# A conditioned linear-attention and MLP block on one core: a new written-out issue order and a new assignment of buffers and PSUM banks

## The chip, the cores and the metric

The kernel runs on one core of one Trainium2 chip. A core has five engines that run beside one another and meet by semaphores: TensorE for matrix products (PE in the profile, its weight loads PEld), VectorE (DVE), ScalarE (ACT), GpSimd (POOL) and SyncE (SP), which here does nothing but issue DMA transfers. The metric is the device time of the program in microseconds, median over the runs; lower is better.

## The reference

The block takes x of 2048 tokens by 512 channels, a condition vector c, and weights. A product of silu(c) with `w_mod` gives six rows of 512 (shift, scale and gate for each half). Cut to what matters:

```python
h = layernorm(x) * (1 + ca) + sa
q, k, v = split(h @ wqkv)                      # 32 heads of 16
phi(t) = [softmax(t @ w_phi), softmax(-(t @ w_phi))]    # 32 features per head
kv = phi(k)^T v ;  z = sum over tokens of phi(k)
o  = (phi(q) kv) / (phi(q) z + 1e-6)
x  = x + ga * (o @ wo)
h  = layernorm(x) * (1 + cb) + sb
x  = x + gb * (gelu(layernorm(h) @ w1 + b1) @ w2 + b2)
```

All in float32. The sums kv and z go over all 2048 tokens, so no token's attention output can be formed before the last token's k and v are known.

## The kernel before, in words

**Precision.** Each large product is made as three products of float32r parts: a high part and a remainder of both operands (function `mm3`). So every operand of a product has a second tile made by a subtraction, `hi` by ACT and `lo` by DVE or POOL.

**Stages.** Tokens are worked in eight blocks of 256, each in two tiles of 128.

1. Start: load the small constants (`blob`), x of blocks 0 and 1 (`xt`), `wkT`, `wqT` and the modulation weights `wm`. `silu_rows` makes the row tile `scp`; `fold_mm` folds `w_phi` into the k and q weights (products `fold`, read by `fold_out` into `wk`, `wq`); `mod_cols` makes the scale and shift columns (`prod`, `affine`); block 0 is transposed by TensorE (`hp`) and becomes `hT`.
2. Per block: products `pk`, `pv` and, for the first three blocks, `pq`. `k_chain` (DVE, ACT, POOL) turns `pk` into softmax features `ek`; `kv_mm` adds their products with `vf` to the bank `pkv`. From block 1 on, h is transposed through DRAM (`nb` to `nt_dram` to `hd`).
3. When all blocks are in: `kv_total` copies `pkv` to `kvT`, `z_total` makes `zp` and the tile `zb`, `kv_blocks` makes the block-diagonal kv.
4. Attention of a block: `attn_e` (features of q, tile `eq`), `attn_a` (`ez` = `eq` times `zb` on POOL, sums `dz`, reciprocals `rd`, then `eq` times `rcq` on POOL), a transpose (blocks 0 and 1 by TensorE products `qp`, items `t`; the others through DRAM, `eb` to `et_dram` to `eT`), products `po` (items `o`), products `pw` (items `w`), layer norms `ln_a`, `ln_b`, `ln_c` on DVE, ACT and POOL (items `la`, `lb`, `lc`), giving `h2`, and a second transpose (blocks 0 and 1 by products `yp`, items `y`; the others through DRAM, `yb` to `yf`), giving `yT`.
5. MLP, in four steps of 512 tokens: eleven products `pg` (item `u`: GELU and copy on ACT, subtraction on DVE, giving `g`), each followed by products into four banks `py0` to `py3` (item `d`), then the output. Attention of later blocks runs between them.

**What sets the order.** No scheduler runs at build time. Function bodies do not issue: a `Held` proxy puts each instruction into a queue of its item and engine (`Later.hold`). The table `ISSUE` then lists, string by string, which queue gives its next instruction (`Later.issue`): `k1.v` is the next DVE instruction of item k1, `+` and `-` name the next or the previous part of the program. Since every engine takes its instructions in the order of issue, the table fixes the order on each of the five engines, SP's DMA queue among them; the semaphore waits follow from the data and from which tile reuses which buffer. All instructions are issued by one line, L218 in the profile.

**Buffers.** `SLOTS["buf"]` says which of 19 equal SBUF buffers each of 284 work tiles uses, `SLOTS["bank"]` which of the eight PSUM banks each of 169 result tiles uses; the short strings choose among two or three copies of small tiles. A tile that reuses a buffer or bank waits until the last reader of the old tile is done. Where two engines read one bank, the one issued later waits for the other.

Of the kernel before, what the change touches and what calls it, by code (L numbers as in the profile page):

```python
# [65 lines left out]
    "den": "10000010",
    "rd": "11010110",
    "st6b0": "10111000",
    "stb0": "01010111",
    "veb0": "01100100",  # L70
    "rsb0": "01110010",
    "st6c0": "11010100",
    "stc0": "11001000",
    "vec0": "00110010",
    "rsc0": "11011010",
    "nmc0": "11110010",
    "st6b1": "11110111",
    "stb1": "00000011",
    "veb1": "10111001",
    "rsb1": "01101110",  # L80
    "st6c1": "11100001",
    "stc1": "01000010",
    "vec1": "10100011",
    "rsc1": "01000111",
    "nmc1": "11011001",
# [3 lines left out]
-init.v -init.v -init.p db.s x0.s x1.s dk.s dq.s dm.s si.a si.v dk.s si.v bd.v si.v dk.s sr.p dq.s s0.v s0.v s0.v  # L89
s0.v s0.v s0.v s0.g sr.a dm.s s1.v s1.v s1.v n0.v s1.v n0.v dm.s s1.v s1.v n0.v s1.g fk.p dm.s ok.a x.s fq.p n0.a  # L90
ok.v fq.p oq.a n1.v n1.v m.v m.g n1.a h0.p dk.s oq.v fk.p m.v m.a n1.v ++x.s fk.p oq.a f.v ok.a oq.v fq.p n1.a ok.v
fq.p f.a m.g m.v f.v h0.p m.v pf.p n1.v m.a m.g n1.s oq.a f.v ok.a dv.s m.v m.g f.a n1.s m.a f.v pf.p n1.s m.v m.v
oq.a n1.s m.a f.v dv.s fk.p m.v ok.v f.a bg.s f.v +x.s pf.p oq.v f.v s.v f.a ok.a f.v vs.a oq.v q0.p s.v s.v s.v s.v
ok.v n1.s q1.p bg.s s.v ++s.v s.g +bg.s vs.a vs.v vs.g n.v ++s.v n.a n.v pf.p n.a n.v n.v pv1.p bg.g ++s.v k0.v n.s
h.a q0.a +s.v n.s h.a +s.v n.s q1.a +bg.g +s.v ++s.v n.s ++s.v k0.v f.a pv0.p ++++x.s h.a +bg.v f.g +bg.s h.a +s.v
+s.v k0.v f.a +bg.s +s.v ++s.v +bg.s k1.v +s.g k1.v f.g
""",
    """
pk1.p n.v -k0.v n.a n.v +s.g e.v bg.a bg.g -k0.a +bg.s +++s.v -n.s pk0.p e.v ++x.s e.g bg.a -v1.a bg.g bg.v +n.v
+n.v k1.v bg.g bg.a -k1.v q0.p +n.a -k1.v +bg.g n.a bg.v +n.a n.v +bg.g +n.v pv1.p h.a k1.v h.a e.g +n.v +bg.a n.v  # L100
++++x.s bg.a e.g ++s.v h.a n.s q1.p -k0.v e.g h.a n.s q0.a n.s f.a ++s.v +n.s f.a f.g k1.v n.s +++s.v +n.s pv0.p
q1.a k0.v f.g e.a +bg.v ++s.v -k1.a k1.v +bg.s ++s.v ++s.v -k0.v -bg.a
""",
    """
pk1.p +++s.v --k0.g --v0.a +s.v ++s.v bg.v -n.s n.s -bg.v n.s +s.g -k0.v -v1.a pv0.p --v0.v --k1.v bg.g ++s.v +n.v
--v1.v bg.v +n.a +++s.v bg.a pv1.p --bg.v bg.a +n.v bg.v -k0.v +n.a e.v -k1.a n.s h.a ++s.v --k1.v pk0.p e.g h.a
k1.v f.a ++s.v --k1.g e.v h.a +++s.v +++s.v -k0.v q1.p f.g -k1.v -k0.a h.a --v1.v k0.v -v0.a +++s.v -v0.v --v0.v
k1.v f.a k1.v -m0.p f.g -m1.p +n.v bg.p q0.p +n.v e.g bg.a q1.a k0.v +n.s +h.a +++s.v k1.v +n.s +h.a +++s.g -k1.v
+n.s e.g v1.v
""",  # L110
    """
pk1.p -k0.v -bg.s -q0.a -e.g n.s -k0.v h.a -q1.s f.a --e.v --k1.g -k0.a -bg.s ----init.v --v1.v --e.a pk0.p n.s k1.v
# [12 lines left out]
""",
    """
pk1.p --k0.g h.a -k1.v -k0.v -k1.a --k1.g h.a -k1.v -v0.a pk0.p ----e.a -k0.v --bg.g f.a k1.v h.a -v0.v k1.v -k0.a
---v1.v -pv1.p k0.v h.a -k0.v f.g f.a +w1.s --bg.a -k1.v f.g -k0.v --v0.a
""",
    """  # L130
pk1.p -k1.v --k0.g ---v0.v --v1.v -k0.v -----e.v -k1.v --k1.g --m0.p -k1.a --m1.p k1.v -m0.p ---v1.v k1.v w1.s
--v1.a -pv1.p --bg.g -k0.v -----e.a -k0.v -k1.v -k0.a -k1.v pk0.p -----e.v -k1.g --v0.v -v1.v ---v0.v +a0.v -v1.v
pv0.p k0.v w1.a -k0.v -v1.a w1.g w1.a -----e.v -k0.v -m1.p k0.v m1.p w1.s w1.g pv1.p v1.v v1.v v0.v d0.s k0.v
-----e.s k0.v k1.v k0.a k1.v -k0.g d0.s v0.a k0.v -pv0.p k1.a v1.a +a0.g k0.v -v0.v k1.v k0.g q1.p -v0.a k1.v w1.a
+a0.v k1.g m0.p m2.p +a0.g m3.p d1.s kT.a +a0.g w1.s q1.a z.p +a0.a w1.g z.a kf.p q1.p z.a kf.v d1.s a0.g --bg.s
q2.p a1.g a0.v +a0.v q0.p a0.v +a0.g a1.v a1.g a0.v q2.p q2.a -v0.v a0.g a1.v a0.g q0.p a0.g a0.v a1.g a1.g a0.g
a1.g a0.g a1.v a0.v q0.a q4.p --bg.s w1.a a1.g +a0.a q1.a +a0.v t00.p a1.g q0.a t01.p t00.a q0.s t00.p +a0.v q4.a
t01.p q4.p a1.g v0.v t01.a q2.a t00.a t01.a +a0.g x0.s x1.s o00.p q2.s o01.p q1.s t10.p o00.a +a0.g t11.p o01.a
o00.v t10.p t11.a t11.p o01.v w00.p t11.a +a0.v t10.a -bg.g t10.a +a0.v o10.p la00.v o11.p +a0.g la00.a --bg.g w01.p
o10.a la00.v o11.a o10.v la00.v o11.v la00.v +a0.g la00.v +a0.g la00.g w2.s w11.p la01.v +lp1.s w1.g +a0.v la01.a  # L140
lb00.v la01.v lb00.v w10.p +a0.g la11.v la01.v lb00.v la11.a la01.v la01.v la01.g q4.a la11.v +a0.g q4.s lb01.v w1.s
q3.p la10.v lb01.v la10.a lb00.v la11.v lb01.v lb00.g la10.v la11.v lb01.v la10.v q3.p lc00.v la11.v lb01.g lc00.a
la11.g la10.v lc01.v la10.v lc01.a la10.g lb11.v +a0.g -bg.a lb10.v q3.a y0.p lb11.v y0.p y0.a lb10.v -bg.g y0.a
y0.v --bg.a y0.v
""",
    """
u0.p -lb11.v -w1.a -lb11.v -lb10.v a0.v -lb11.g u0.p a0.v -lb10.v -lc11.v a0.v a0.s -lb10.g -lc11.a -w2.g a0.s u0.p
-lc10.v a0.v -lc10.a a0.s a1.v -q3.a a0.s -y1.p a1.v a0.s -y1.p -y1.a u0.p -w1.g a0.s -y1.a -y1.v a0.s -y1.v a0.s
u1.p -q3.s ---bg.g u1.p u.a u.a a0.s u1.p u.v -w1.s u.a a1.g -w2.s u.a a0.s -w2.a a1.g d.p u.v d.p u.a a1.g u1.p u.a
a1.g d.p -w2.g a1.a d.p d.p a1.a a1.v d.p a1.g d.p a1.v d.p u.a u.v o00.p u.a a1.v o01.p -w1.a a1.g u.v u.p o01.a  # L150
+lp0.s x0.s o00.a o01.v a1.v -w2.g o00.v d.p a1.v d.p w00.p -w2.a a1.g +a0.v a1.g a1.g a1.v a1.g a1.g d.p la00.v
w01.p la00.a u.a la00.v a1.g +a0.v a1.v u.a d.p +a0.g a1.v d.p la00.v +a0.g a1.v a1.s d.p a1.v a1.s d.p +a0.g +a0.a
la00.v a1.s la01.v u.p la00.v a1.s la00.g la01.a +a0.g a1.s la01.v a1.s u.v -w2.g a1.s la01.v lb00.v d.p a1.s u.a
lb00.v d.p u.a la01.v la01.v d.p la01.g -w2.s u.p +a0.g lb01.v +a0.a a1.s u.v a1.s +a0.v x1.s -w1.g lb01.v d.p u.a
lb01.v lb00.v d.p lb01.v lb00.v +a0.v lb00.g -w2.s d.p -w2.s lb01.g d.p lc00.v -w2.g +a0.v lc00.a u.p u.a lc01.v
lc01.a u.v +a0.v -w2.a y0.v +a0.g o10.p u.a y0.v o11.p y0.s d.p o10.a y0.s o11.a o10.v d.p -w2.g y0.s o11.v w10.p
# [1013 lines left out]
```

## Time and profile before

| | |
|---|---|
| Median of the runs | 467.67 us (467.45 to 468.56, three runs) |
| Profiled execution, first to last instruction | 466.6 us; its own time is not given beside it, and the median is 1.07 us longer than this span |
| Granted TensorE clock | 1.000 |
| PE busy | 458.5 us, 98% of the span, 3297 instructions |
| DVE, POOL, ACT busy | 317.1, 279.7, 234.6 us |
| DMA | 68.05 MB, mean 146 GB/s |

A busy engine in the profile is one with an instruction in flight. For PE this overlaps: a 128x512 product is listed with 391 ns, but twelve of them follow one another in 2.72 us. So the share of PE says that it is rarely without work, not how much could be saved in it; the list of its waits says what it stood still for. The waits of the other engines cost nothing unless PE comes to wait for them.

### The profile page before, as it was taken

The numbers are of one execution on the slowest core, as the hardware profiler recorded it, in microseconds if no ns is written. First come the engines' busy times: TensorE is split into PE (matmuls) and PEld (weight loads), VectorE is DVE, ScalarE is ACT, GpSimd is POOL, SyncE is SP. The second block draws the span as 40 slices with busy tenths as digits, with TensorE's granted clock in tenths as the row PEclk, the third lists the DMA queues.
The fourth block names the chain that finished last, engine by engine and source line by source line (L and its number), as shares of the span: only waits on it lengthen the run. The fifth ranks groups of instructions, "written<-read, shape, count | busy, mean of one in ns | idle before, by whom it ended". The sixth has DMA issues, their size and how long they took to land.

```text
span 466.6 us, 8536 instructions
## 1 busy us (share of the span) xinstructions
PE 458.5 (98%) x3297; PEld 372.3 (80%) x3297; DVE 317.1 (68%) x612; ACT 234.6 (50%) x381; POOL 279.7 (60%) x233
## 2 busy tenths in 40 slices
PE   8999999999999999999999999999999999999996
PEld 5887888888878878978787878787788788788884
DVE  5999999989938599389797579896484472221113
ACT  4757866767440827848537743176133234422221
POOL 2369587999799998989899684756721020300000
PEclk9999999999999999999999999999999999999999
DMA  8998738492372664836837728077445504000003
GB/s 311 382 311 301 195 84 276 95 269 55 100 257 95 189 209 90 244 104 139 224 135 160 225 53 241 1 130 178 143 90 136 122 14 93 15 30 1 1 1 135
DMA packets 83673, 68.05 MB, mean 146 GB/s; under 512 B 54688, under 2 KB 70960, under 8 KB 83376
## 3 DMA queue, kind: packets, MB, share of 16 engines
q1 hardware_dynamic: 83632, 67.50, 50.9%
q8 instruction: 26, 0.43, 0.4%
q14 instruction: 15, 0.12, 0.1%
HBM read 44.94 MB, written 22.55 MB: 145 GB/s over the span
## 4 chain that ended last, share of the span: by engine, by line
PE 85%; DMA 5%; DVE 4%; POOL 2%; issue 1%; ACT 1%; SPq 0%; DVEq 0%; POOLq 0%; ACTq 0%
PE py L218 25%; PE pg L218 24%; PE pv L218 8%; PE pk L218 8%; PE pw L218 8%; PE pq L218 7%; PE pkv L218 2%; DMA wm<-in_wmodT 2%; PE po L218 1%; DVE pw L218 1%; DMA eT<-et_dram 1%; DMA wms<-in_wmodT 1%; DMA xt<-in_x 1%; PE qp L218 1%; POOL w2a L218 1%
## 5 line engine op out<-in xcount | busy, mean ns | idle before, releaser
L218 PE MATMUL pg<-yT,w 128*128 128x512 f32 (+1 forms) x528 | 115.3, 371 | 0.6 <-DVE yT L218 0.3
L218 PEld LDWEIGHTS pg<-yT,w 128*128 128x128 f32 x528 | 92.8, 188 | 18.5 <-DVE yT L218 0.5
L218 ACT ACTIVATE pg<-pg,blob 128x512 f32<-128x512 f32 x44 | 29.1, 662 | 100.6 <-PE pg L218 100.4
L218 PE MATMUL py<-w2a,g 128*128 128x512 f32 x288 | 70.7, 391 | 0.0
L218 DVE TENSOR_TENSOR g<-pg,g 128x512 fp32r<-128x512 f32 x40 | 27.2, 680 | 61.7 <-ACT g L218 61.7
L218 PEld LDWEIGHTS py<-w2a,g 128*128 128x128 f32 x288 | 53.6, 188 | 12.6 <-issue 1.6
L218 PE MATMUL pk<-wk,hT 128*128 128x512 f32 x192 | 46.2, 392 | 0.8 <-ACT hT L218 0.7
L218 PE MATMUL py<-w2b,g 128*128 128x512 f32 x192 | 46.9, 391 | 0.0
L218 PE MATMUL pv<-wvh,hT 128*128 128x512 f32 x192 | 45.9, 392 | 0.0
L218 PE MATMUL pw<-wo,oT 128*128 128x512 f32 x192 | 45.4, 390 | 0.0
L218 PE MATMUL pq<-wq,hT 128*128 128x512 f32 x192 | 45.3, 391 | 0.0
L218 PEld LDWEIGHTS pk<-wk,hT 128*128 128x128 f32 x192 | 35.6, 188 | 9.1 <-ACT hT L218 1.1
L218 PEld LDWEIGHTS py<-w2b,g 128*128 128x128 f32 x192 | 35.9, 188 | 8.1 <-issue 0.7
L218 PEld LDWEIGHTS pw<-wo,oT 128*128 128x128 f32 x192 | 35.9, 188 | 7.8 <-issue 0.4
L218 PEld LDWEIGHTS pv<-wvh,hT 128*128 128x128 f32 x192 | 35.7, 188 | 7.5
L218 PEld LDWEIGHTS pq<-wq,hT 128*128 128x128 f32 x192 | 35.8, 188 | 7.3
L218 POOL TENSOR_TENSOR ez<-eq,zb 128x1024 f32<-128x1024 f32 x15 | 36.8, 2469 | 5.5 <-ACT last L218 3.0
L218 POOL TENSOR_TENSOR yT<-yf,yT 128x256 fp32r<-128x256 f32 x24 | 17.2, 742 | 35.1 <-ACT yT L218 35.0
L218 POOL TENSOR_TENSOR ek<-ek,rck 128x1024 f32<-128x1024 f32 x16 | 30.8, 1939 | 4.5 <-DVE rck L218 2.3
L218 POOL TENSOR_TENSOR eq<-eq,rcq 128x1024 f32<-128x1024 f32 x15 | 28.9, 1937 | 0.3
L218 ACT ACTIVATE g<-pg 128x512 fp32r<-128x512 f32 x40 | 24.0, 599 | 9.5 <-PE pg L218 4.4
L218 DVE TENSOR_REDUCE smq<-eq 128x64 f32<-128x1024 f32 x16 | 19.2, 1207 | 6.8 <-ACT eq L218 6.8
(153 smaller groups left out, 783.4 us busy)
## 6 DMA issues: line engine op xcount, KB each, us to landing
et_dram<-eb SPq DMA_DIRECT2D x48, 128.0 KB, 2.9
eT<-et_dram SPq DMA_DIRECT2D x12, 512.0 KB, 5.1
xt<-in_x SPq DMA_DIRECT2D x8, 512.0 KB, 6.1
wms<-in_wmodT SPq DMA_DIRECT2D x8, 512.0 KB, 5.9
x<-in_x SPq DMA_DIRECT2D x8, 512.0 KB, 5.2
out<-x SPq DMA_DIRECT2D x15, 256.0 KB, 2.5
nt_dram<-nb SPq DMA_DIRECT2D x28, 128.0 KB, 3.4
hd<-nt_dram SPq DMA_DIRECT2D x7, 512.0 KB, 5.5
```

The source lines that it names most:

```text
L218: return lambda *a, **k: self.later.hold(self.letter, lambda: f(*a, **k))
```

## The change

Only the tables `SLOTS` and `ISSUE` change. The functions, the operations, their shapes, their engines and the number of buffers stay. The build of the change has the same products in number and size; their order, that of the other engines' instructions and of the DMA issues is new throughout, and so are nearly all buffers and banks. Its description: same operations; order of issue and buffers worked out anew by a search that knows PSUM readers, measured landings and rows of small products.

```diff
 SLOTS = {
...
     "bank":
-    "1264710140570135353253136162435026621304533162143502472521023727652170445605353123554624602715375317"
-    "153573175304761253153253215213576546037217123132712723327513246406462",
+    "0264053314155425735412536467370270221442034761733163556365177342730773725615173601336026023171451745"
+    "514174546406415225332755375372361602361271477554171417636207331133131",
...
 ISSUE = [
     """
-init.v -init.v -init.p db.s x0.s x1.s dk.s dq.s dm.s si.a si.v dk.s si.v bd.v si.v dk.s sr.p dq.s s0.v s0.v s0.v
+-init.v x0.s -init.v -init.p db.s x1.s dq.s dm.s dk.s dk.s dk.s dk.s s0.v si.a dm.s si.v si.v s0.v s0.v dq.s s0.v
...
-+a0.v k1.g m0.p m2.p +a0.g m3.p d1.s kT.a +a0.g w1.s q1.a z.p +a0.a w1.g z.a kf.p q1.p z.a kf.v d1.s a0.g --bg.s
+m3.p q1.p kT.a d1.s -bg.g d0.s z.p +a0.g z.a +a0.g kf.p z.a q1.p kf.v q1.a a0.g q2.p q1.a a1.g a0.v ----v1.v a0.v
```

Three places in the order, before and then in the change.

SP, the first rows of its DMA queue (`blob` the small constants, `xt` a block of x, `k` and `q` the weights to fold, `wm` the modulation weights, `wv_s` the v weights). Before:

```order
L218 DMA blob<-in_small 128x217
L218 DMA xt<-in_x 128x2x512 x2
L218 DMA k<-in_wkT 128x512
L218 DMA q<-in_wqT 128x1024
L218 DMA wm<-in_wmodT 128x1024
L218 DMA k<-in_wkT 128x512 x2
L218 DMA q<-in_wqT 128x1024
L218 DMA wm<-in_wmodT 128x1024 x3
```

The change:

```order
L216 DMA xt<-in_x 128x2x512
L216 DMA blob<-in_small 128x217
L216 DMA xt<-in_x 128x2x512
L216 DMA q<-in_wqT 128x1024
L216 DMA wm<-in_wmodT 128x1024
L216 DMA k<-in_wkT 128x512 x4
L216 DMA wm<-in_wmodT 128x1024
L216 DMA q<-in_wqT 128x1024
L216 DMA wm<-in_wmodT 128x1024 x2
```

The constants now go behind the first block of x, the first half of the q weights goes ahead of all k weights, and the four pieces of the k weights go ahead of the second `wm`. On PE the first fold products are accordingly those of q.

PE, where block 0 is transposed for the MLP (`yp`), between the last `pw` products and the first `pg`. Before:

```order
L218 MATMUL pw<-wo,oT_470 128x512
L218 MATMUL pq<-wq,hT 128x512 x24
L218 MATMUL yp<-blob,h_438 128x128 x8
L218 MATMUL pg<-yT_475,w_376 128x256
L218 MATMUL pg<-yT_477,w_376 128x256
```

The change:

```order
L216 MATMUL pw<-wo,oT_470 128x512
L216 MATMUL pq<-wq,hT 128x512 x12
L216 MATMUL yp<-blob,h_438 128x128 x8
L216 MATMUL pq<-wq,hT 128x512 x12
L216 MATMUL pg<-yT_475,w_376 128x256
L216 MATMUL pg<-yT_477,w_376 128x256
```

Twelve of the twenty-four `pq` products moved from ahead of the transposes to behind them. In the same way, as the two `m3.p` lines of the diff show, twelve `pq` products (`q1.p`) now stand between the last `pkv` products and `zp`.

POOL, from the attention of block 0 to the last `eq` times `rcq` of block 1 (`ez` are the products with `zb`, `dz`, `den` and `rcq` the small steps of the denominators). Before, from the third `ez` on:

```order
L218 TENSOR_TENSOR ez<-eq,zb 128x1024
L218 TENSOR_TENSOR dz<-dz,rcq 128x128
L218 TENSOR_TENSOR den<-dz 128x64
L218 TENSOR_TENSOR den<-den,deps 128x64
L218 TENSOR_TENSOR dz<-dz,rcq 128x128
L218 TENSOR_TENSOR den<-dz 128x64
L218 TENSOR_TENSOR rcq<-rcq,rd 128x128
L218 TENSOR_TENSOR den<-den,deps 128x64
L218 TENSOR_TENSOR eq<-eq,rcq 128x1024
L218 TENSOR_TENSOR rcq<-rcq,rd 128x128
L218 TENSOR_TENSOR eq<-eq,rcq 128x1024 x2
L218 TENSOR_TENSOR ez<-eq,zb 128x1024 x2
```

The change, from behind the third `ez`:

```order
L216 TENSOR_TENSOR dz<-dz,rcq 128x128
L216 TENSOR_TENSOR den<-dz 128x64
L216 TENSOR_TENSOR den<-den,deps 128x64
L216 TENSOR_TENSOR ez<-eq,zb 128x1024
L216 TENSOR_TENSOR dz<-dz,rcq 128x128
L216 TENSOR_TENSOR rcq<-rcq,rd 128x128
L216 TENSOR_TENSOR eq<-eq,rcq 128x1024
L216 TENSOR_TENSOR den<-dz 128x64
L216 TENSOR_TENSOR den<-den,deps 128x64
L216 TENSOR_TENSOR ez<-eq,zb 128x1024
L216 TENSOR_TENSOR rcq<-rcq,rd 128x128
L216 TENSOR_TENSOR eq<-eq,rcq 128x1024 x2
```

The two `ez` products of block 2, which stood behind the last `eq` times `rcq` of block 1, now stand ahead of it, on either side of the one of block 0. A subtraction `w_377` that stood ahead of the first `ez` has moved behind this piece.

More of the change, by code (lines that the diff above doesn't have):

```diff
@@ L82 @@
[L82 to L85, printed above, removed]
+    "0264053314155425735412536467370270221442034761733163556365177342730773725615173601336026023171451745"
+    "514174546406415225332755375372361602361271477554171417636207331133131",
+    "st6a": "00000000",
+    "sta": "00000100",
+    "vea": "00000000",
+    "rsa": "00001011",
+    "nma": "00000111",
+    "dz": "001111111",
+    "mxk": "1010111011101110",
+    "smk": "1000000000100101",
+    "rck": "0011001000100101",
@@ new lines @@
+    "mxq": "00001001",
+    "smq": "00000000",
+    "rcq": "01000000",
+    "den": "00000000",
+    "rd": "00000000",
+    "st6b0": "00000000",
+    "stb0": "00000000",
+    "veb0": "00000000",
+    "rsb0": "00000000",
+    "st6c0": "00000000",
+    "stc0": "00000000",
+    "vec0": "00000000",
+    "rsc0": "00000000",
+    "nmc0": "00000000",
+    "st6b1": "00000000",
+    "stb1": "00000000",
+    "veb1": "00000000",
+    "rsb1": "00000000",
+    "st6c1": "00000000",
+    "stc1": "00000000",
+    "vec1": "00000000",
@@ L86 @@
+    "rsc1": "00000000",
+    "nmc1": "00000000",
 }
@@ new lines @@
++a0.s d.p yf0.g yf1.a d.p yf1.a yf0.g yf1.a d.p out.v yf1.a d.p yf1.g d.p out.s yf1.g
+""",
+    """
+a0.s a1.a -yf1.g -yf1.g u.p a1.v a1.g u.p +a0.v u.a u.a +a0.v a1.g -out.v u.p a1.v u.a -out.s a0.s u.a a1.v -xb.g
+u.v d.p u.v u.a x0.s d.p a0.s u.a +a0.g d.p u.v d.p +a0.g a1.v d.p a0.s +a0.g +a0.a -out.v d.p +a1.v d.p xb.g a0.s
+d.p +a1.v d.p u.p a1.g a1.g a1.g a1.v a1.g +a0.g d.p u.a d.p u.a a1.g d.p u.v d.p -out.v +a0.a +a0.v o00.p a1.g
+o01.p +a0.v d.p o01.a d.p +a0.g o00.a +a0.v d.p a1.v u.p a1.v +a0.g +a0.v a1.s a1.s a1.v a1.s u.p u.a o01.v a1.s u.a
@@ new lines @@
+la10.v +a0.s d.p la10.v +a0.s la10.v la11.v d.p +a0.s la11.v u.p la11.v la10.v la11.g y0.s la10.g +a0.s lb10.v +a0.s
++a0.s lb10.v u.p lb10.v lb10.v lb10.g lc10.v la11.v lc10.a lb11.v u.a u.p u.a lb11.v yf0.a +a0.s lb11.v yf0.a lb11.v
+u.a lb11.g +x0.s xb.g lc11.v u.a u.v lc11.a u.v d.p y1.v d.p y1.v d.p +a1.g +a1.a y1.s d.p y1.s +a1.a d.p +a1.v
++a1.g y1.s d.p y1.s +a1.v d.p +o00.p u.a +a1.v +a1.g +o01.p u.a +a1.v d.p u.a u.a y1.s d.p u.a u.a u.a +x1.s +o00.a
+d.p u.v yf0.g +o01.a +o00.v d.p yf0.g yf0.a d.p +o01.v yf0.g d.p out.v d.p out.v +w01.p out.s out.v +a1.v yf1.a
@@ new lines @@
+yf1.a yf1.a yf1.a +a1.g yf0.a +w00.p +a1.g +a1.g yf1.g yf1.g yf1.g d.p +la00.v yf1.g out.v yf0.g
+""",
+    """
+u.p la00.v la00.v la00.v la00.v la00.v u.p la00.g u.a a1.v u.a a1.g u.v a1.g u.p u.a a1.g u.a u.v lb00.v u.p u.a
+lb00.v u.a lb00.v la01.v u.v la01.v d.p la01.v u.a d.p u.a la01.v a1.v d.p a1.v d.p a1.v a1.s d.p a1.v a1.s d.p
+-out.s u.v a1.s d.p la01.v la01.v la01.g a1.s d.p lb01.v a1.s d.p a1.s lb01.v d.p a1.s a1.s d.p d.p a1.s u.p a1.s
+d.p u.a d.p u.a d.p u.v d.p lb00.v lb00.g d.p lc00.v lb01.v lc00.a lb01.v d.p lb01.g d.p lc01.v y0.v lc01.a o11.p
@@ new lines @@
+yf0.a d.p yf1.g d.p yf0.g d.p d.p d.p out.v d.p out.v d.p out.s +u.p out.v -out.s out.v --out.s out.s out.s -out.s
+""",
+    """
+u.p -out.s u.a u.a u.v d.p u.a d.p u.a d.p u.v d.p u.p d.p u.a d.p u.a d.p u.v d.p d.p d.p d.p d.p u.p u.p u.a u.a
+u.v d.p u.a d.p u.a d.p u.v d.p d.p d.p u.p u.p u.a u.a u.v d.p u.a d.p u.a d.p u.v d.p d.p d.p d.p d.p d.p d.p u.p
+u.p u.a u.a u.v u.p u.a u.a u.v u.p u.a u.a u.v d.p u.a d.p u.a d.p u.a u.a d.p u.a u.a u.a d.p u.v d.p d.p d.p d.p
+d.p d.p d.p out.v d.p out.s d.p out.v ---out.s d.p out.s d.p out.v d.p out.s out.v out.v out.s out.s
```

186 lines of the change are left out of this document (68 added, 118 removed).

## The prediction

> **What bounds the kernel now.** I read the engine totals first, then the chain that ended last, then the list of what PE waited for.
>
> ```profile
> PE 458.5 (98%) x3297; PEld 372.3 (80%) x3297; DVE 317.1 (68%) x612; ACT 234.6 (50%) x381; POOL 279.7 (60%) x233
> PE 85%; DMA 5%; DVE 4%; POOL 2%; issue 1%; ACT 1%; SPq 0%; DVEq 0%; POOLq 0%; ACTq 0%
> 39.77 2.72 PE pq L218 x12
> ```
>
> PE is in 85% of the chain, and the third line, a piece of that chain, shows its pace: twelve products of 512 columns in 2.72 us. The change has the same products, so at this pace PE's work is the same, and a new order can gain only what PE now waits. That is the whole of this list (waited for: us in total, times, longest):
>
> ```profile
> PE warm L218 <- DVE mhalf L218: 0.9, 1, 0.9
> PE fold L218 <- DMA k<-in_wkT: 0.9, 1, 0.9
> PE pk L218 <- ACT hT L218: 0.7, 1, 0.7
> PE zp L218 <- ACT kvT L218: 0.6, 1, 0.6
> PE pg L218 <- DVE yT L218: 0.3, 1, 0.3
> PE pg L218 <- ACT yT L218: 0.3, 1, 0.3
> PE po L218 <- DMA eT<-et_dram: 0.2, 1, 0.2
> PE pk L218 <- POOL hT L218: 0.2, 1, 0.2
> ```
>
> The sum is 4.1 us. The first 0.9, ahead of the warming products, waits for the program's first memsets, which stay; 3.2 us are open to an order, 0.7% of the run. Against them stands that any of the many tight meetings of five engines may now miss. The two stretches where these are tightest, grouped (us, then PE, PEld, DVE, ACT, POOL busy with instruction counts, clock, DMA share, GB/s):
>
> ```profile
> 120.00:160.00 40.00, 39.45 (x518) 32.23 (x517) 25.13 (x34) 17.16 (x27) 36.95 (x26) 1.00 0.44 151
> 160.00:200.00 40.00, 39.12 (x274) 33.22 (x273) 31.36 (x63) 27.54 (x40) 37.27 (x30) 1.00 0.65 187
> ```
>
> POOL has only 3 us free in each 40, so here its order matters nearly as much as PE's. The clock is full, so no term below comes from it.
>
> **The change part by part. The start.** Issues, landings and first users (start, length, what; the last two rows are landing times of the two tiles, min/median/max):
>
> ```profile
> 0.74 0.40 SPq L218 DMA_DIRECT2D blob<-in_small  x1
> 1.19 4.54 DMA xt<-in_x
> 2.68 0.43 SPq L218 DMA_DIRECT2D q<-in_wqT  x1
> 2.85 0.21 ACT L218 ACTIVATE ex<-blob 128x4 f32<-128x4 f32 x1 [0.83 <-DMA blob<-in_small]
> 3.96 0.15 DVE L218 TENSOR_TENSOR sc<-blob,rx 128x4 f32<-128x4 f32 x1
> 5.76 1.29 DVE L218 BATCH_NORM_STATS2 st6a<-xt 128x6 f32<-128x512 f32 x2 [1.64 <-DMA xt<-in_x]
> 5.86 1.05 PE L218 MATMUL scp<-blob,sc 128*128 128x128 f32 x8
> 7.78 1.16 PE L218 MATMUL fold<-bd,k 128*128 128x128 f32 x8 [0.86 <-DMA k<-in_wkT]
> DMA to landing us min/median/max: 2.1/2.1/2.1
> DMA to landing us min/median/max: 6.3/7.3/8.3
> ```
>
> Before, `blob` lands at 0.74 + 2.1 = 2.8, and `sc` is ready at 4.1, well ahead of PE, which is warming until 5.86. In the change `xt` is issued first: it lands about 1.19 - 0.74 = 0.45 earlier, at 5.3, and `blob` behind it at about 5.5. From its landing to `sc` it took 4.1 - 2.8 = 1.3, and DVE now has one of the two statistics (0.65) in between: `scp` starts at about 7.4, a new wait of 1.5, and ends at 8.5. The first q weights landed at 2.68 + 6.3 = 9.0; without the k piece ahead of them they land at about 8.3, so the folds go on without another wait at 8.5, where before they began at 7.78: 0.7 lost. After that the four k pieces come in one row and the waits of 0.7 and 0.2 for `hT` should shrink, because `hd` of block 1 no longer stands behind three weight loads. But both `hp` tiles now share one bank, and the second must wait for the last reader of the first:
>
> ```profile
> 17.61 0.42 DVE hT L218
> ```
>
> That reader ended at 18.0 before; PE would want the bank at about 17.4. I take 0.7 lost + 0.2 for the bank - 0.9 of old waits = **0.0**, with -0.9 (blob is small and lands with xt) to +1.3 (both new waits in full, the old ones too) as bounds.
>
> **zp.** The twelve `pq` products put between `pkv` and `zp` last 2.72; what PE waited for is one ACT copy:
>
> ```profile
> 135.66 1.99 PE L218 MATMUL zp<-kvT,blob 128*128 128x256 f32 x8 [0.55 <-ACT kvT L218]
> ```
>
> It is covered four times over: **-0.6**. If the cover were gone, the 0.6 would be back.
>
> **The two `ez` ahead of block 1's last product.**
>
> ```profile
> 138.61 4.78 POOL L218 TENSOR_TENSOR ez<-eq,zb 128x1024 f32<-128x1024 f32 x2
> 153.91 3.83 POOL L218 TENSOR_TENSOR eq<-eq,rcq 128x1024 f32<-128x1024 f32 x2
> 157.70 4.72 POOL L218 TENSOR_TENSOR ez<-eq,zb 128x1024 f32<-128x1024 f32 x2
> 158.64 1.09 PE L218 MATMUL po<-qT,gab 64*32 64x256 f32 x32
> 159.67 1.97 PE L218 MATMUL qp<-blob,eq 128*128 128x128 f32 x16
> ```
>
> `eq` of block 1 was ready at 157.74 and PE transposed it (`qp`) at 159.67: 1.9 us of slack. Now 4.7 us of `ez` go first. PE comes sooner by the 0.6 of `zp` and by half of the `po` group (0.5), which goes behind the first transpose. If POOL gained nothing elsewhere, PE would wait 4.7 - 1.9 + 1.1 = 3.9 us, of which the 1.1 is only time already gained: net +2.8. On the other side POOL reaches `ez` earlier, since the 2.4 us subtraction `w_377` and others moved behind, and `zb` comes 0.6 sooner; then the slack nearly holds and the cost is 0. I take **+0.4**, nearer the second because the moved subtraction alone is half of the 4.7.
>
> **yp and the first pg.**
>
> ```profile
> 161.39 3.00 PE L218 MATMUL pw<-wo,oT 128*128 128x512 f32 x12
> 165.79 0.70 DVE L218 BATCH_NORM_STATS2 st6b<-pw 128x6 f32<-128x512 f32 x1 [0.66 <-ACT x L218]
> 176.46 1.62 ACT L218 ACTIVATE h<-pw,nmc,rsc 128x512 f32<-128x512 f32 x2 [1.11 <-DVE nmc L218]
> 179.08 1.04 PE L218 MATMUL yp<-blob,h 128*128 128x128 f32 x8
> ```
>
> From the end of the first `pw` (164.4) to the end of `h` (178.1) the layer norms took 13.7. In the change PE has 1.1 of `po`, three `pw` of 2.72 and one `pq` of 2.72 in that time, 12.0, so an unchanged chain would make `yp` wait 1.7. The chain is shorter now: DVE issues the statistics ahead of ACT's copy of the same bank, which saves the 0.66 shown, and block 1's first steps no longer stand ahead of block 0's last ones; I put it at 12.4, a wait of 0.4. Behind `yp` the other `pq` group covers both waits of `pg`, 0.6. **-0.2**, from -0.6 to +1.1.
>
> **eT of block 2.**
>
> ```profile
> 193.29 6.65 DMA eT<-et_dram
> ```
>
> Its second half stood on SP behind a `w1s` and a `ws` load; in the change the two halves are issued in a row, so 2 us of landing go. The DVE transposes that feed them now stand behind two subtractions for `yT`, which eats most of it. **-0.2**, to +1.0 if they are late.
>
> The MLP steps, where PE waited for nothing, get **0.0**. Sum: 0.0 - 0.6 + 0.4 - 0.2 - 0.2 = -0.6. The span of the profiled execution is 466.6, the median 1.07 longer; a wait that goes shortens both alike, so the forecast is 467.67 - 0.6 = **467.1 us**, no change that can be told: what a measurement of this kernel can tell from none is about 0.3%, 1.4 us.
>
> **The rivals.** *Nearly all waits go.* For it: each wait on PE's list has been given a visible cover, and my new waits come from landings put together by hand. Against it: the start's `blob`. Of the 3.2 us some 0.4 stays: 467.67 - 2.8 = 464.9.
>
> *Banks come back too soon, slower.* In the bank string, read along PE's order, an up product `pg` takes or gives a bank with only 2.72 us of other products between last write and reuse in ten places or more; before, in one. What must happen in that time:
>
> ```profile
> L218 ACT ACTIVATE pg<-pg,blob 128x512 f32<-128x512 f32 x44 | 29.1, 662 | 100.6 <-PE pg L218 100.4
> L218 ACT ACTIVATE g<-pg 128x512 fp32r<-128x512 f32 x40 | 24.0, 599 | 9.5 <-PE pg L218 4.4 <-POOL wlast L218 2.7 <-PE pw L218 1.3
> L218 DVE TENSOR_TENSOR g<-pg,g 128x512 fp32r<-128x512 f32 x40 | 27.2, 680 | 61.7 <-ACT g L218 61.7
> L218 ACT ACT_TABLE_LOAD x16 | 20.5, 1283 | 1.0 <-PEq L1163 0.7
> ```
>
> 0.66 + 0.60 + 0.68 = 1.94, so 0.8 is to spare: enough on an idle ACT, not when a table load of 1.28 stands ahead, which costs PE 0.5. The rival decides from the point where four of these places meet one: 4 x 0.5 = +2.0, 469.1 us. Queued behind the waiting `pg` are then all of PE and every later `py`. Against it: ACT is busy only half of the time. [...] No run so far shows a wait of this kind.
>
> *POOL is late.* The bound of +2.8 in place of +0.4 at `eq`: 467.1 + 2.4 = 469.5. It holds if POOL cannot fill earlier gaps.
>
> *The order does nothing*, new waits for old ones one for one: 467.7.
>
> **How the numbers follow.** Forecast 0.45, own range 466.0 to 468.4; a fifth of it (0.09) lies below 466.27, the rest (0.36) within 0.3%. Nearly all waits go: 0.28, faster. Banks: 0.12, slower. POOL: 0.09, slower. Nothing: 0.06, same. So faster 0.37, same 0.42, slower 0.21. The range, 464.6 to 469.6, takes in the rivals' times and leaves out a new stall of more than 2 us.
>
> **What would show it.** Right: no `zp` and no `pg <- yT` on PE's list; `scp` starting near 7.4; a wait of `qp` or its weight load for POOL `eq` under 1 us; PE's waits summing to about 3.5. Wrong: `scp` still at 5.9 and the list under 1.5 us (the gain), `pg`, `py` or `pw` waiting for DVE `g` or `x` in the MLP steps (the banks), or `po` waiting for `eT` after 200 us by more than 1 us at a time, which I have priced at nothing.

## The result, and the profile after

The changed kernel takes 478.21 us (median of four runs, 477.22 to 480.5); the kernel before took 467.96 us beside it (467.45 to 468.56). The ratio is 1.0228, with a 95% interval of 1.0201 to 1.0255: about 10 us slower, outside the range of the prediction and on the other side of its forecast. The profiled execution took 477.91 us, its span is 476.1 us, 9.5 more than before.

The same two lines of the page as quoted before, for the changed kernel: busy time per engine, then the share of each engine in the chain that ended last.

```profile
PE 461.0 (97%) x3297; PEld 372.7 (78%) x3297; DVE 323.1 (68%) x612; ACT 234.7 (49%) x381; POOL 280.3 (59%) x233
PE 69%; POOL 6%; DMA 3%; issue 2%; DVE 1%; SPq 1%; ACT 0%; DVEq 0%; POOLq 0%
```

The products are the same 3297, but PE's share of the chain fell from 85% to 69%: other engines now set the pace for part of the span. What PE waited for (us in total, times, longest):

```profile
PE pk L216 <- issue: 2.3, 1, 2.3
PE fold L216 <- DMA q<-in_wqT: 1.6, 1, 1.6
PE qp L216 <- POOL eq L216: 1.5, 1, 1.5
PE pv L216 <- issue: 1.5, 1, 1.5
PE po L216 <- DMA eT<-et_dram: 1.1, 2, 0.7
PE pkv L216 <- issue: 1.1, 1, 1.1
PE warm L216 <- DVE mhalf L216: 0.9, 1, 0.9
PE scp L216 <- PE warm L216: 0.6, 1, 0.6
PE pv L216 <- POOL hT L216: 0.3, 1, 0.3
PE pkv L216 <- POOL ek L216: 0.2, 1, 0.2
PE hp L216 <- DVE hT L216: 0.2, 1, 0.2
```

The list sums to 11.3 us against 4.1 before, +7.2. Three kinds of loss are in it. The largest, 4.9 us in three pieces, has "issue" as its releaser: PE waited for nothing that the profile shows. The start lost 1.3 (`fold` and `scp`, 2.2 against 0.9). `qp` waits 1.5 for POOL, and `po` 0.9 more for `eT`. Gone are, as predicted, the waits of `zp` (0.6) and of `pg` for `yT` (0.6); the 0.9 of `pk` for `hT` went too, and three small waits, 0.7 together, came. A fourth loss is not in the list but in the clock. The stretch behind the wait of `qp`, grouped (us, busy times, and the granted clock after the busy times):

```profile
160.00:168.00 8.00, 6.48 (x66) 4.72 (x64) 3.59 (x4) 3.00 (x6) 7.69 (x9) 1.00 0.70 244
168.00:172.00 4.00, 4.00 (x32) 3.51 (x17) 1.84 (x3) 2.63 (x5) 4.00 (x3) 0.57 1.05 389
```

The trace's record of the clock has 3.41 us at half clock there, and that gives a mean of 0.57 over 4 us. If PE does nothing but products in that time it loses by estimate half of the 3.41, 1.7 us; in the run with 108 below, twelve `pv` products that ran from 87.57 us over such a stretch took 4.60 us, where twelve at full clock take 2.88. With it the sum is 7.2 + 1.7 = 8.9 of the 9.5 us.

**The three stalls without a cause.** They all fall in or right behind rows of `pkv`, the small products. PE's timeline round the first (start, length, what, and the idle time before it):

```profile
108.48 2.88 PE L216 MATMUL pv<-wvh,hT 128*128 128x512 f32 x12
111.29 1.85 PE L216 MATMUL pkv<-ek,vf 128*17 128x32 f32 x192
115.44 1.88 PE L216 MATMUL pk<-wk,hT 128*128 128x512 f32 x7 [2.30 <-issue]
```

A row of 192 such products has as many weight loads, 384 instructions in 1.8 us, 4.7 ns each; twelve large products are 24 instructions in 2.72 us, 113 ns each. The page's list of DMA queues has one of the kind `instruction`:

```profile
q8 instruction: 26, 0.43, 0.4%
```

These are 26 transfers of 16 KB each, and PE's 6594 products and loads are 25.8 times 256. In the trace a transfer of this queue begins at 112.70, 130.91 and 135.82 us, each 0.2 to 1.0 us ahead of a stall. So I counted PE's products, loads and semaphore instructions in the order of the trace. The stalls come at the places 2241, 2753 and 3009, 512 and 256 apart, and I looked at every 256th place from them. This is my count, not a view of the profile:

```
place in    reached   us since the place   next instruction
PE's order  at, us    256 earlier          at, us
1729         99.92    4.2                   99.93
1985        111.82   11.9                  111.83
2241        112.95    1.1                  115.44   stall
2497        129.88   14.4                  129.88
2753        131.44    1.6                  133.33   stall
3009        136.84    3.5                  138.09   stall
before, the shortest: 2753 at 127.52, 3.8 us since 2497, no stall
```

All three stalls stand exactly at such a place, and only where 256 instructions were used up in 3.5 us or less; the next instruction came 3.45 to 4.8 us after the place before. In each of the three the next instruction came 2.3 to 2.7 us after the transfer had begun. In the kernel before, whose rows of `pkv` stand otherwise to these places, the shortest block of this stretch lasted 3.6 to 3.8 us (the count is good to one instruction, and one is worth 0.2 here), and it has no such stall. The theory for the experiments, an estimate from this table: PE's instructions come in blocks of 256, the next block is asked for when one has been begun, it takes about 3.5 us to come, and a block that lies wholly in `pkv` is used up sooner.

**Where POOL's lateness comes from.** PE at `zp` and at `qp`, and POOL's row between them, in the changed kernel:

```profile
141.73 1.89 PE L216 MATMUL zp<-kvT,blob 128*128 128x256 f32 x8
167.18 0.55 PE L216 MATMUL qp<-blob,eq 128*128 128x128 f32 x3 [1.52 <-POOL eq L216]
```
```profile
144.38 8.11 POOL L216 TENSOR_TENSOR ez<-eq,zb 128x1024 f32<-128x1024 f32 x3 [3.46 <-issue]
153.62 2.41 POOL L216 TENSOR_TENSOR ez<-eq,zb 128x1024 f32<-128x1024 f32 x1
160.42 2.41 POOL L216 TENSOR_TENSOR ez<-eq,zb 128x1024 f32<-128x1024 f32 x1
163.30 3.83 POOL L216 TENSOR_TENSOR eq<-eq,rcq 128x1024 f32<-128x1024 f32 x2
```

POOL stood idle 3.46 us until `zb` was there; this "issue" is a wait for the two ACT copies of `zp`, which ran from 142.8 to 144.3 (before, they ended at 138.3, 0.3 ahead of the first `ez`). The prediction's rows of before give the difference: `ez` begins at 144.38 instead of 138.61, 5.8 late; `eq` of block 1 ends at 167.1 instead of 157.7, 9.4 late, the other 3.6 being the two `ez` of block 2 that now go first. Of the 9.4 the old slack of 1.9 takes its part, and PE goes on at 167.18 instead of 159.67, 7.5 late. So the stalls are one part of a delay that runs through POOL, and PE's list of waits shows only where the parts come to the surface.

### The profile page after: what moved, and what is told of

Its sections match the earlier page's. It is cut to its first block, busy times and chain, and to the rows that moved or that the text cites. A ratio compares the mean times of both kernels' runs of the same rounds, so it can differ in the third digit from the quotient of the medians.

```text
span 476.1 us, 8581 instructions
## 1 busy us (share of the span) xinstructions
PE 461.0 (97%) x3297; PEld 372.7 (78%) x3297; DVE 323.1 (68%) x612; ACT 234.7 (49%) x381; POOL 280.3 (59%) x233
## 4 chain that ended last, share of the span: by engine, by line
PE 69%; POOL 6%; DMA 3%; issue 2%; DVE 1%; SPq 1%; ACT 0%; DVEq 0%; POOLq 0%
PE pg L216 23%; PE py L216 23%; PE pw L216 9%; PE pv L216 5%; PE pk L216 4%; POOL ez L216 3%; DMA eT<-et_dram 2%; PE pkv L216 2%; PE po L216 2%; POOL eq L216 1%; PE pq L216 1%; DMA et_dram<-eb 1%; POOL ek L216 1%; PE qp L216 1%; SPq L216 1%
## 5 line engine op out<-in xcount | busy, mean ns | idle before, releaser
L216 PE MATMUL py<-w2a,g 128*128 128x512 f32 x288 | 68.8, 390 | 0.0
L216 POOL TENSOR_TENSOR rsb<-veb,mhalf 128x1 f32<-128x1 f32 x16 | 8.7, 548 | 38.0 <-DVE veb L216 37.9
L216 ACT ACTIVATE h<-pw,nmc,rsc 128x512 f32<-128x512 f32 x16 | 12.3, 778 | 35.8 <-DVE nmc L216 27.2
```

The costliest lines, as they stand in the source:

```text
L216: return lambda *a, **k: self.later.hold(self.letter, lambda: f(*a, **k))
```

## The experiments

Each kernel has its own runs of the kernel before beside it; the ratios are to these. 1% is 4.7 us.

**Do the stalls follow the count?** In the kernel before the third warming product is replaced by tiny ones, so that all later PE instructions move by 108 or by 56 places and nothing else changes.

```diff
-    for _ in range(3):
+    for _ in range(2):
         nc.tensor.matmul(warm, ones.to_broadcast([P, P]), ones.to_broadcast([P, 512]), start=True, stop=True)
+    for _ in range(28):      # 15 in the other run
+        nc.tensor.matmul(warm[:32, :2], ones.to_broadcast([P, 32]), ones.to_broadcast([P, 2]), start=True, stop=True)
```

> The kernel before, with the third warming product (4 PE instructions, 1.7 us) replaced by 28 tiny ones (112 instructions): every later PE instruction stands 108 places further on, nothing else changes. Theory (blocks of 256 instructions): in the changed kernel PE stood still at instructions 2241, 2753 and 3009 of its stream, 256 or 512 apart, each time less than 1 us after a 16 KB transfer of the instruction queue had begun; between that point and the one 256 instructions earlier only 1.1, 1.6 and 3.5 us had passed, and the next instructions came 3.45 to 4.8 us after the earlier point. Worked out with 3.45 us for all of before's rows of pkv, this shift puts two block ends into four of its rows of 384 instructions: PE loses 11 us, 477 to 482 us. Rival (the stalls come from something else at those times, such as data or transfers): the tiny products are hidden at the start and the time stays within 1 us of before, 467 to 469.

> The same edit with 15 tiny products: every later PE instruction stands 56 places further on. Theory (blocks of 256 instructions): worked out the same way, no row of pkv then holds a whole block, so no stall: 467.5 to 468.5 us, as before. Rival (more instructions or a shorter warming cost by themselves, in proportion): about half of what the shift by 108 costs.

Measured: moved by 108, 488.47 us, ratio 1.0425 (1.0395 to 1.0455); moved by 56, 469.15 us, 1.0022 (1.0008 to 1.0037). The waits of the first:

```profile
PE pkv L218 <- issue: 11.0, 4, 3.9
PE po L218 <- DMA eT<-et_dram: 1.5, 1, 1.5
```

Four stalls of 11.0 us in sum, as worked out, at places 1472, 1984, 2496 and 3265 of the count, 256 or a multiple of it apart and, to one instruction, on the same grid as those of the changed kernel. The whole loss is larger, 20.5 us. Behind each of the four the granted clock was 0.57 to 0.59 over 4 us; the first of them:

```profile
84.00:88.00 4.00, 1.92 (x156) 1.69 (x142) 1.05 (x3) 4.00 (x8) 4.00 (x3) 1.00 0.02 4
88.00:92.00 4.00, 4.00 (x12) 3.12 (x11) 3.92 (x11) 1.97 (x3) 4.00 (x3) 0.57 0.50 80
```

Four times the estimated 1.7 us is 6.8; the tiny products also ran later than the one that they replaced (`scp` began at 7.7 instead of 5.9, 1.8 us). 11.0 + 6.8 + 1.8 = 19.6 of the 20.5. The shift by 56 has no stall and costs 0.2%, not half of the other, so the number of instructions is not the cause: where the blocks of 256 end is.

One part of the theory does not hold, that a block used up in less than 3.5 us always brings a stall. In the run with 108 the whole block of the places 705 to 960 is this row, used up in 1.26 us, and PE went on without a pause:

```profile
65.68 1.33 PE L218 MATMUL pkv<-ek,vf 128*32 128x32 f32 x128
```

There a 16 KB transfer had begun at 62.62, 3.1 us ahead of the block. At the four stalls the transfer began 1.0 to 3.0 us after the block had been begun. Over all stalls of this kind in these runs the next instruction came 2.2 to 2.8 us after the transfer's start, 3.6 in the one of `after_shift180` below. So the blocks are shown, by eight stalls in three kernels on one grid of 256 places (three in the changed kernel, four here, one in `after_shift180`), and the time from a transfer's start to the next instruction; what decides when a transfer starts stays open.

**Two parts of the change put into the kernel before.** First the twelve `pq` products between the last row of `pkv` and `zp`, then block 2's two `ez` ahead of block 1's last `eq` on POOL, then both.

```diff
 # PE
-pkv  zp  kvp  pq x12
+pkv  pq x12  zp  kvp
 # POOL
-eq<-eq,rcq x2  ez x2
+eq<-eq,rcq  ez x2  eq<-eq,rcq
```

> The kernel before with one part of the change alone: twelve pq products stand between the last pkv row and zp. Theory: zp no longer waits 0.6 to 0.7 us for kvT, but zb is ready 2 us later, so POOL's row to eq of block 1 ends 2 us later, and the 1.9 us of slack at qp are used up, PE being there 0.7 us sooner: a wait of qp of 0.5 to 1 us, total 467.5 to 468.5 us, no gain. Rival (my prediction's step: the cover is free): 467.0 to 467.4 us, no wait of qp.

> The kernel before with another part of the change alone: on POOL the two ez of block 2 (4.7 us) go ahead of block 1's last eq*rcq. Theory: POOL has no gap there, so this eq is ready 4.7 us later, at 162.4 instead of 157.7; PE wants it at 159.7: a wait of 2.7 us at qp and what follows from it, 470.5 to 472 us. Rival (POOL or the products around it make room): a wait under 1 us, 467.5 to 468.5.

> The kernel before with both parts of the change together: twelve pq products between the last pkv row and zp, and block 2's two ez ahead of block 1's last eq*rcq. Theory (one row of POOL work from zb to eq, in which delays add): eq of block 1 is ready 1.7 to 2 us plus 4.7 us later, about 164.3; PE comes to it at about 159.1 and waits 4.5 to 5.5 us, with 3.4 to 6.8 us at half clock behind it: 474 to 476.5 us. Rival (the two delays cover one another): no more than the larger of the two alone, 471 to 473.

Measured: `zp` late 470.05 us, 1.0049 (1.0028 to 1.0070); `ez` first 472.45, 1.0099 (1.0067 to 1.0131); both 473.65, 1.0111 (1.0093 to 1.0129). The wait of `qp` in the first, the second, and the third kernel:

```profile
PE qp L218 <- DVE eq L218: 1.9, 1, 1.9
```
```profile
PE qp L218 <- POOL eq L218: 2.5, 1, 2.5
```
```profile
PE qp L218 <- DVE eq L218: 1.9, 1, 1.9
PE qp L218 <- POOL eq L218: 1.2, 1, 1.2
```

`zp` no longer waits, and the kernel is about 2 us slower: what was won at `zp` (0.6) came back threefold at `qp`, 1.9, more than the 0.5 to 1 that I had put down, because DVE's `eq` of block 0 hangs on `zb` too and PE wants it first. The two `ez` bring a wait of 2.5 us, where the working gave 2.7. The profiled run of this kernel took 473.61 us, 5.9 more than the kernel before; the other 3.4 are by estimate what the clock behind the wait gives, 0.57 over 8 us, twice the length seen in the changed kernel:

```profile
161.00:169.00 8.00, 6.68 (x25) 5.98 (x26) 2.95 (x4) 2.17 (x4) 6.88 (x6) 0.57 0.49 183
```

Together the two parts cost no more than can be told from the larger alone: 1.11% against a sum of 1.48%. The first wait of 1.9 covers part of the second, 1.2 instead of 2.5. The theory that the delays add is wrong; the rival holds, and its 471 to 473 would be 472 to 474 against the 468.65 us of before in these runs.

**The stalls taken out of the changed kernel.** In two ways by breaking up the rows of `pkv`, once by a shift of 180 places ahead of them.

```diff
 # PE, after_split
-pkv x3 tiles  pk1  pk0  pv0  pv  pv  pkv x3 tiles  pv1  pkv x3 tiles
+pkv x1  pk1  pkv x2  pk0  pv  pv  pkv x2  pv0  pkv x1  pv1  pkv x3 tiles
 # PE, after_split2
+pkv x1  pk1  pkv x2  pk0  pv0  pv  pv  pkv x1  pv1  pkv x2  pq x12  pkv x3 tiles  zp
 # PE, after_shift180
+45 tiny products (180 instructions) into pv's bank ahead of the pv before the first of these rows
```

> The changed kernel with two places of PE's order altered so that no block of 256 instructions falls wholly into pkv products: the two pkv tiles of block 5 go behind the product pk1 of block 7, and pv0 of block 7 goes between the second and third pkv tile of the next row. Theory (blocks): the three stalls of 2.3, 1.7 and 1.2 us go, PE reaches zp about 5 us sooner; POOL, busy without a pause up to 140.9, follows by only some 3.5, so the wait of qp for eq grows from 1.5 by up to 1.7: 473 to 475.5 us. Rival (the stalls belong to that time or to the transfers in it): 477 to 479.

> The changed kernel with its last three pkv rows broken up in another way: pk1 of block 7 between the first and second tile of one row, pv1 of block 7 between the first and second tile of the next, and the twelve pq products that stood behind the last row ahead of it. No block of 256 instructions then falls wholly into pkv. The 2.7 us of pv0 stay where they were, so that PE comes to the later pv banks no sooner than by the stalls that went. Theory (blocks): no idle time of PE without a visible cause; of the 5.2 us about 1 to 2.5 come back as waits for DVE's reading of pk (0.8 was seen) and 0.7 as zp's wait for kvT; qp's wait does not shrink: 474.5 to 477 us. Rival (DVE's k chain is what bounds this stretch, the stalls only hide it): all comes back as waits for DVE ek: 477.5 to 479.5.

> The changed kernel in its own order, with 45 tiny products (180 instructions, about 0.7 us) ahead of the product pv that precedes the row of pkv at 111 us: the ends of the blocks of 256 instructions then fall 180 places earlier. Theory (blocks): the stalls at the first two of the three rows (2.3 and 1.7 us) go and one of about 2.3 us stands in the third row. If nothing else were late there: 1 us gained, 477; if PE without its stalls meets DVE's reading of pk and ACT's of pv as in the runs with broken rows: the waits for these appear in place of the stalls and the time stays at 477.5 to 479. Rival (stalls tied to a place or a time, not to a count): the stalls stay where they were.

Measured: 479.35 us, 1.0242 (1.0201 to 1.0283); 478.54, 1.0221 (1.0178 to 1.0265); 478.33, 1.0228 (1.0204 to 1.0252). None can be told from the change's 1.0228. The first two have no stall of this kind left on PE's list, and other waits in their place. The second, without its lines of the start and of `po`:

```profile
PE qp L216 <- POOL eq L216: 1.4, 1, 1.4
PE pq L216 <- ACT vf L216: 1.3, 1, 1.3
PE pq L216 <- ACT qs L216: 1.2, 2, 0.9
PE pk L216 <- DVE ek L216: 0.8, 1, 0.8
PE pv L216 <- ACT vf L216: 0.7, 1, 0.7
PE pv L216 <- DVE ek L216: 0.6, 1, 0.6
PE zp L216 <- ACT kvT L216: 0.6, 1, 0.6
```

Without `qp` and `zp` that is 4.6 us, nearly the 4.9 of the stalls: PE wants the banks of `pk`, `pv` and `pq` before DVE and ACT have read them. `after_split` waits 4.1 us for DVE's `ek` in two such places. The third kernel moved the stalls, as the count says: none at the first two rows, one in the third, longer than the 2.3 us expected, and at place 3264 of the count.

```profile
132.68 1.57 PE L216 MATMUL pkv<-ek,vf 128*17 128x32 f32 x154
137.91 0.51 PE L216 MATMUL pkv<-ek,vf 128*17 128x32 f32 x38 [3.65 <-issue]
```

Behind it the clock was 0.60 from 138 to 142 us. The waits for DVE and ACT that I had expected in place of the stalls did not come; the largest in this stretch is 0.7 us for POOL's `ek`. Still the time stayed, and so far the rival could hold, that the other engines bound this stretch and the stalls only hide it.

**Both late causes of `zb` together.** The shift, and the twelve `pq` products that stood between the last row and `zp` inside that row; then this second edit alone.

```diff
 # PE
-pv x12  pkv x3 tiles  pq x12  zp
+pv x12  pkv x1  pq x12  pkv x2  zp
```

> The changed kernel with the 180 tiny instructions, and with the twelve pq products that stood between the last row and zp put inside that row, behind its first tile; zp and kvp follow the row at once. By the count no block of 256 instructions then lies wholly in pkv, and zb waits for no pq. Theory (the stalls and zp's place together made zb late): zb is ready 2 to 3.5 us sooner, POOL with it, and the wait at qp goes down by as much: 475 to 476.5 us. Rival (the banks that pq and pk need, or POOL's own row, set the pace): the time stays at 477.5 to 479.5 with new waits for ACT or DVE in place of the stalls.

> The changed kernel with the twelve pq products inside the last pkv row, behind its first tile, and without the 180 tiny instructions of the run that gained 1.1%. By the count the stalls stay at the first two of the three rows (2.3 and 1.7 us) and the one in the last row goes. Theory (the stalls make zb late, and POOL's row from zb to eq sets when PE goes on): zb is 1.5 to 3 us later than in the run with both edits, so about half of its gain is left: 475.5 to 477 us against a kernel before at 468 to 468.6. Rival A (only zp's place mattered): the whole gain stays, 473 to 474.8. Rival B (only the stalls mattered): nothing stays, 477.5 to 479.

Measured: both, 474.64 us, 1.0120 (1.0093 to 1.0146); the second alone, 477.96, 1.0202 (1.0170 to 1.0233). PE in the first of them, from the tiny products to `zp`:

```profile
108.46 0.93 PE L216 MATMUL pv<-ones 128*32 128x2 f32 x90
109.32 3.02 PE L216 MATMUL pv<-wvh,hT 128*128 128x512 f32 x12
112.27 1.85 PE L216 MATMUL pkv<-ek,vf 128*17 128x32 f32 x192
114.05 5.76 PE L216 MATMUL pk<-wk,hT 128*128 128x512 f32 x24
119.64 8.32 PE L216 MATMUL pv<-wvh,hT 128*128 128x512 f32 x36
127.89 1.91 PE L216 MATMUL pkv<-ek,vf 128*17 128x32 f32 x192
129.74 2.99 PE L216 MATMUL pv<-wvh,hT 128*128 128x512 f32 x12
132.66 0.73 PE L216 MATMUL pkv<-ek,vf 128*17 128x32 f32 x64
133.48 3.06 PE L216 MATMUL pq<-wq,hT 128*128 128x512 f32 x12
136.46 1.32 PE L216 MATMUL pkv<-ek,vf 128*17 128x32 f32 x128
138.33 1.99 PE L216 MATMUL zp<-kvT,blob 128*128 128x256 f32 x8 [0.55 <-ACT kvT L216]
```

There is no stall and no wait of 0.1 us or more but `zp`'s for `kvT`; `zp` begins at 138.33 instead of 141.73 with the same products done, and POOL's `ez` at 141.1 instead of 144.4. 1.08 points of the 2.28 are won back, about half of the loss. The time is a little better than the theory gave, and `zb` comes as much sooner as it said; but the wait at `qp` did not shrink:

```profile
PE qp L216 <- POOL eq L216: 1.5, 1, 1.5
```

PE comes to `qp` 3.3 us sooner (163.90 instead of 167.18) and finds POOL as late behind it as before. The two kernels differ by nothing but the 180 tiny instructions, more work for PE, and the one that has them is 0.82 points, 3.8 us, faster, each against its own runs of the kernel before; the intervals do not meet. So stalls do cost time: in this order two of them, 3.6 us on PE's list, cost about 3.8 us. That the changed kernel itself, with three, loses as much of its 10 us to them is likely, but no run shows it in its own order. That `zp`'s place alone gives 0.26 points cannot be told from nothing (1.0202 against 1.0228): of the forecasts for the second edit alone that of rival B came out, nothing stays, and the theory's, that half of the gain stays, did not. The runs that moved or removed stalls before this one gained nothing; their lists show waits for banks, or a longer stall with a slow clock behind it, that their edits brought.

**POOL's order taken back, and `zp` put back.** Four tries in the changed kernel, and `after_pool` once more in the order of `after_split2`.

```diff
 # after_zfirst, PE            # after_zfirst2: also buf of the second ez  g -> 8
-pkv  pq x12  zp  kvp
+pkv  zp  kvp  pq x12
 # after_pool, POOL            # after_pool2: also buf of block 0's qT  2 -> h
-... ez(2) ... ez(2) ... eq<-eq,rcq x2
+... eq<-eq,rcq x2  ez(2) x2
```

> The changed kernel with the twelve pq products put back behind zp and kvp, as they stood before. Theory: these 2.7 us delayed zp and so the tile zb, for which POOL's first ez waited 3.5 us; POOL's row from ez to eq then starts 2.7 us sooner, the wait of 1.5 us of qp for eq goes, and with it the 3.4 us at half clock behind it (about 1.8 us); the wait of 0.6 to 0.7 of zp comes back: 475 to 476.5 us. Rival (the two ez ahead of eq are what makes qp wait): qp still waits over 1 us, 478 to 479.

> The run with zp ahead of the twelve pq products once more, with the second ez in a buffer that no pq product reads (in the first run that ez waited 2.65 us for pq because of its buffer, so POOL got nothing of the time won). Theory (POOL's row from zb to eq is what PE waits for): the row ends 2 us sooner after the last pkv, the 1.5 us at qp go but for 0.7 of zp: 476 to 477.5 us. Rival (zp's place does not matter): 478 to 479, qp waiting over 1 us.

> The changed kernel with the two ez of block 2 put back behind block 1's eq*rcq on POOL, as before, and the two DVE sums that read them with them. Theory (these two ez, 4.7 us, are what makes qp wait): eq of block 1 is ready 4.7 us sooner, the wait of 1.5 us and the half-clock stretch behind it (about 1.8 us) go: 474.5 to 476 us. Rival (POOL is late because zb is): the row from the first ez on is late anyway and the wait stays over 1 us: 477 to 479.

> The run with block 2's ez behind block 1's eq once more, with qT of block 0 in a buffer that no ez has used (in the first run qT had to wait 5.6 us for the sum over that ez). Theory: eq of block 1 is ready 3.6 us sooner, no wait at qp: 475.5 to 477 us. Rival (something else is as late as POOL there): another wait of 1 us or more near 167 us, 478 to 480.

> Both of the edits before together. If both theories hold and the two costs are apart, the two gains add: 470.5 to 473.5 us. If the stretch is bounded by DVE, only the gain of the POOL order shows: 474.5 to 476.5.

Measured: 478.41 us, 1.0215 (1.0165 to 1.0264); 480.94, 1.0284 (1.0249 to 1.0318); 482.58, 1.0318 (1.0273 to 1.0364); 483.18, 1.0336 (1.0314 to 1.0357); with `after_split2`'s order 482.07, 1.0289 (1.0259 to 1.0319). None gained. `after_zfirst` came out as its rival said, with `qp` still waiting 1.4 us, and `after_pool2` met another wait in the place that its rival named, but a longer one; the others left both forecasts. A row each: POOL in `after_zfirst`, then PE's largest wait in `after_pool` and in `after_pool2`.

```profile
148.72 5.65 POOL L216 TENSOR_TENSOR ez<-eq,zb 128x1024 f32<-128x1024 f32 x2 [2.65 <-PE pq L216]
```
```profile
PE po L216 <- ACT qT L216: 5.6, 1, 5.6
```
```profile
PE pw L216 <- DVE oT L216: 4.8, 1, 4.8
```

With `zp` first POOL began its first `ez` 3.5 us after the last `pkv` instead of 5.5, but the second lies in a buffer that `pq` still reads. With that buffer changed it waited 5.09 us, for what the profile does not name; this stays open. With POOL's order taken back, `qT` waits for the sum over the `ez` whose buffer it takes, and with that buffer changed DVE's `oT` waits behind that sum in DVE's own order. In both the wait of `qp` is gone, and a longer one stands behind it. The order of POOL, of DVE and the buffers hang together, and in none of these tries could one be set back alone at a gain. So the 3.6 us that the two `ez` cost in the changed kernel are read from its POOL rows, and their price is shown only in the kernel before (0.99%).

## Why the prediction was wrong

**"The change has the same products, so at this pace PE's work is the same."** This step failed first. The products are the same, but the instructions of PE also have to arrive, and where 256 of them fall into a row of small products they did not: 4.9 us of gaps at three places; the pair of runs that differs only in the shift puts two such gaps at about 3.8 us of time. No term of the sum and no rival had it. The evidence was in the profile of before: 26 transfers of 16 KB in the instruction queue, PE rows of 4.7 ns an instruction, and a shortest block of 3.6 to 3.8 us in the stretch of `pkv`.

**zp, "covered four times over: -0.6".** The wait went as said, but the step priced only PE's side of what it moved. `zb` was taken to come 0.6 us sooner and came 6.0 later (144.3 instead of 138.3), of which 2.7 are these products. Alone this part costs about 2 us (0.49%).

**The two ez, +0.4 with a bound of +2.8.** The upper bound was near the wait: 2.5 us when done alone. The lower one, POOL gaining time by the subtraction moved away, was chosen because that subtraction is half of the 4.7; POOL gained nothing since it waited 3.46 us for `zb` anyway. The trace of before already set a limit: `zb` was ready at 138.3 and POOL began the first `ez` at 138.61, so moving work away could win 0.3 us there, 0.9 with a `zb` that comes 0.6 sooner, and not 2.4. The rival "POOL is late" had the mechanism right for these two products and gave 469.5; done alone in the kernel before, with the clock behind the wait, they make it 472.45.

**"The clock is full, so no term below comes from it."** True of before. Behind some of the waits that the new orders brought the granted clock was 0.57 over 4 us, in `before_ez` over 8, which by the estimate from the clock's record costs 1.7 us more in the changed kernel, 3.4 in the profiled run with `ez` first and 6.8 in the shift by 108.

**The start, 0.0 within -0.9 to +1.3.** `scp` began at 6.09 instead of the forecast 7.4, with a wait of 0.6 instead of 1.5; the folds began at 8.83, forecast 8.5. The waits of `pk` for `hT` (0.9) became 0.3 for `pv` and 0.2 for `hp`. +1.3 - 0.9 + 0.5 = +0.9, inside the bounds.

**yp and pg, -0.2.** Both waits of `pg` for `yT` are gone, 0.6, and `yp` does not wait: the better bound.

**eT, -0.2 with +1.0 as bound.** `po` waits 1.1 instead of 0.2, +0.9: the bound.

**The MLP, 0.0, and the rival of the banks.** Right: no `pg`, `py` or `pw` of the MLP waits for a bank anywhere in the list, though banks come back after 2.72 us of products in ten places or more. The waits for banks that were seen are the 0.2 us of `hp`, which the prediction had, and those in orders that I made, in the stretch of `pk` and `pv` (up to 3.3 us in `after_split`).

PE's list and the clock account for 7.2 + 1.7 = 8.9 of the 9.5 us of the span, but they say where PE lost time, not what each part of the change is worth. Shown by runs are that stalls cost time (the pair, and the shift by 108) and, in the kernel before, the price of `zp`'s place (0.49%) and of the two `ez` (0.99%), which overlap (1.11% together). How the other half of the 10 us, which no run won back, divides between `ez`, the clock, the start and `eT` stays open.

## What to carry to other kernels

Count instructions, not only time: where PE has long rows of tiny products, mark every 256th instruction of its stream and see how fast each block of 256 is used up: in the kernel before the shortest of the stretch of `pkv` took 3.6 to 3.8 us and had no stall, those in front of the changed kernel's stalls took 1.1 to 3.5. Not each block that short stalls (one of 1.26 us did not), but all stalls of this kind here stood behind one. A few instructions more ahead of such rows cost 4.2% in one kernel here and won 0.8 points in another, so a new order has to be compared over several such shifts before it is called better or worse. When work is moved to cover a wait, follow what now comes later on every engine to the next place where PE needs it. Where an order and its buffers were found together, setting one of them back is no fair test of it: here it brought longer waits of its own, up to 5.6 us.

## What the runs showed that was not expected

A kernel became 0.82 points faster by 180 more instructions (1.0202 to 1.0120), and another 20 us slower by 108 more at its start, by which the first product behind them came only 1.8 us later.

Behind standstills of PE of 1.5 to 4 us the granted clock was often 0.57 to 0.60 over the next 4 us (the four stalls of the shift by 108, `qp` in the changed kernel, the stall of `after_shift180`), in `before_ez` 0.57 over 8. It is not so behind each: of the five standstills of over 1 us in the changed kernel's profile only that at `qp` has it, and that of 1.9 us at `qp` in `before_zlate` does not: the mean clock of its profiled run is 1.000. What decides behind which standstill the clock is lower no run here tests.
